# Splitting the even row frequencies once more in a gated attention and spectral mixer, with folds through PSUM, gates on ScalarE and another search of the order

## The chip, the cores and the metric

The kernel runs on one core of a Trainium2 chip. The metric is the device time of one execution in microseconds (us); the number given for a kernel is the median of its runs. A profile is one further execution under the hardware profiler.

## The reference, cut to what matters

```python
x = A_x                                   # (1, 2048, 640), float32
g = sigmoid((x * gate_w).sum(-1, keepdims=True))
# a: 32 heads of 20, each position looks at itself and 7 earlier ones, 2 apart
qkv = x @ A_wqkv                          # 640 -> 1920
logits = q . k[pos - 2*w] * 20**-0.5      # w = 0..7
a = (softmax(logits) @ v[pos - 2*w]) @ A_wo
# b: filter in the 2-D frequency domain
b = irfft2(rfft2(x, axes=(-2, -1)) * (B_w_r + 1j * B_w_i), s=(2048, 640))
out = g * a + (1 - g) * b
```

## The kernel before, in words

The position s is 16 p + j, with p on the 128 partitions and j = 0..15. Attention couples only positions of the same parity of j, so there are two parities of everything.

**The order of the work** is not written out. Every operation goes through `Plan.record` (line 222), which notes what it reads and writes, and a cost. `Plan.order` (line 278) then makes a fixed order for all engines by a list schedule forwards and backwards, and repeats it `AGAIN` = 100 times with the operations' priorities moved at random, each name of a tile by one amount over the whole program; it keeps the best by its own estimate. Because all instructions are issued from one place, the profile gives them all one line, L639, and a reader goes by the names of tiles.

**Stages.** 

- *qkv* (line 703): for 16 positions j and 4 groups of heads, 15 matmuls of 480 or 482 columns (three products of split high and low halves for each of five slices of 128 channels) into a PSUM bank from `BP`, seven banks in turn. ScalarE evicts a bank into `ev` (two buffers, each for two j) and a store to `qkvd` in HBM follows. For the first group of heads, ScalarE also copies the column `z`, the gate's argument. The very first product (`qkv<-st`) is in plain single precision from tiles `st0` (x, then the first slice of the weights), `st1`, `st2` (the other slices); `load_x` and `load_chunk` (lines 674 to 701) load them.
- *fold* (line 824): the spectral branch first folds x along the 640 channels, so that even and odd frequencies, and cosines and sines, are separate products of half the length. Each of eight folds takes two j (`fx`, with a scratch tile `fe`): six operations with both operands in SBUF, folds 0 to 6 on VectorE, fold 7 on GpSimd. The results are stored to HBM (`fd`) and come back later (`f`).
- *cols* (line 849): products with `fc`, the transform along p, into `z`, copied into `zg`.
- *attend* (line 743), two halves for each of 8 units by parity: VectorE multiplies q and k windows (`pr`, the q copied into PSUM by ScalarE as `qbank`) and reduces (`L`), a softmax, GpSimd multiplies with v windows (`pv`), VectorE reduces (`o`), and SyncE stores `od`.
- *gates* (line 735): `g`, `ng` and `nng`, three small tiles of 128 x 16, from `z`.
- *freq* (line 871), 16 groups g of row frequencies: `zc` is gathered from `zg`; `v` and `u` are products with the channel transform `bt`, three matmuls each, of 321, 161 and 160 columns; `ab` is their sum and difference; `xa` to `xd`, the transform along j; the product with the filter `wp`; the sums `s`; and `g`, back along j, into `zg`.
- *project_even* (line 1078): `ot` is read back, transposed (`oTp`, `oT`) and multiplied with `wo` (`woa` and `wob`, 15 matmuls each); results to HBM (`ad`).
- *spatial* (line 996): for each j, `o1` and `o2` (`oa`, `ob` in the profile), products with `gt`, back along the channels: three matmuls each, of 322, 161 and 161 columns; then `ha`, `hb` along p. For even j VectorE forms y from `ha`, `h`, and `yi` is added on GpSimd.
- *project_odd* (line 1094): for odd j, y from `ho` by five operations on GpSimd (`ODD_POOL`, line 1136), then the projection `woa`, `wob` and its addition. These projections come last; they need the attention of the odd parity.

Of the kernel before, what the change touches and what calls it, by code (L numbers as in the profile page):

```python
# [16 lines left out]
S, D = 2048, 640  # L17
# [7 lines left out]
PERM = np.array([0, 320] + list(range(2, 320, 2)) + list(range(1, 320, 2)))  # L25

BP = (0, 1, 2, 3, 4, 5, 6)
BV, BU, BX, BG, BO = (0,), (1, 2), (3, 4), (5,), (6,)
# [3 lines left out]
def dft_tables():  # L32
# [7 lines left out]
    ke, ko = PERM[:161], PERM[161:]  # L40
    kb = PERM[2:161]
# [9 lines left out]
    def half(n, *ends):  # L51
# [3 lines left out]

    bt = np.zeros((640, 642))
    bt[0:161, 0:161] = np.cos(tau * np.outer(np.arange(161), ke) / D) * half(161, 0, 160)
    bt[161:321, 161:321] = np.cos(tau * np.outer(np.arange(160), ko) / D) * half(160, 0)
    bt[321:480, 323:482] = -np.sin(tau * np.outer(np.arange(1, 160), kb) / D)
    bt[480:640, 482:642] = -np.sin(tau * np.outer(np.arange(1, 161), ko) / D) * half(160, 159)  # L60
    bt = np.concatenate(
        [bt[0:128, 0:161], bt[128:256, 0:321], bt[256:384, 161:482], bt[384:512, 321:642], bt[512:640, 482:642]], 1
    )

    j, k2 = np.arange(16), np.arange(16)
    md = np.zeros((16, 16, 2, 4, 2, 16, 4))
    mf = np.zeros((16, 2, 16, 4, 16, 2, 4))
    for g in range(16):
        for a in range(4):
            th = tau * np.outer(j, 4 * g + a + 128 * k2) / 2048  # L70
# [48 lines left out]
    d = np.arange(161)  # L119
# [5 lines left out]
    gt[0:161, 0:161] = np.cos(tau * np.outer(ke, d) / D) * ck(ke)  # L125
    gt[161:321, 161:322] = np.cos(tau * np.outer(ko, d) / D) * ck(ko) * (d < 160)
    gt[321:480, 322:483] = -np.sin(tau * np.outer(kb, d) / D) * ck(kb) * ((d > 0) & (d < 160))
    gt[480:640, 483:644] = -np.sin(tau * np.outer(ko, d) / D) * ck(ko) * (d > 0)
    gt = np.concatenate(
        [gt[0:128, 0:161], gt[128:256, 0:322], gt[256:384, 161:483], gt[384:512, 322:644], gt[512:640, 483:644]], 1  # L130
    )
    f = np.float32
    return {
        "t_fc": np.concatenate([fc, back[0].T, back[1].T], 1).astype(f),
# [21 lines left out]
class Plan:  # L156
# [121 lines left out]
    def order(self):  # L278
# [26 lines left out]
        for _ in range(AGAIN):  # L305
            move = MOVE * rng.choice([0.3, 1.0, 2.0]) * rng.normal(size=len(names))
            move *= rng.random(len(names)) < rng.choice([0.1, 0.5, 1.0])
            for op, t in zip(ops, (best[1] + move[family]).tolist()):
                op.tail = t
# [162 lines left out]
TURNS, AGAIN, MOVE, SEED = 6, 100, 2.0, 2  # L472
# [33 lines left out]
class Mixer:  # L506
# [17 lines left out]
    def places(self, pp, dr, sb):  # L524
# [35 lines left out]
        self.yr, self.yir = ring("raw3", "raw4", "e0", "ya"), n("f", 2)  # L560
# [10 lines left out]
    def work(self):  # L571
# [14 lines left out]
        self.qkv(0, 0)  # L586
# [4 lines left out]
        self.qkv(1, 0)  # L591
        for hg in (1, 2, 3):
            self.load_w(None, hg)
            self.qkv(0, hg)
# [13 lines left out]
        self.bt, self.gt = self.one("bt", 1288, tag="e0"), self.one("gt", 1288, tag="e1")  # L608
        S.dma_start(self.bt[:, 0:1284], ins["t_bt"])
# [16 lines left out]
        p.chain = ""  # L626
        staged([self.spatial(j) for j in range(1, NJ, 2)], 2)
# [75 lines left out]
    def qkv(self, par, hg, between=None):  # L703
# [3 lines left out]
        for jj in range(8):  # L707
            j = 2 * jj + par
            hi, lo = self.xT[j]
            b = self.ps(BP, f"qkv{u}_{jj}")  # L710
# [113 lines left out]
    def fold(self, q):  # L824
        p = self.p
        G = p.dve if q in FOLD_DVE else p.pool
# [4 lines left out]
        e = self.er.next(f"fe{q}", 2, 321)  # L831
        f, o = xt[:, :, 0:640], xt[:, :, 0:321]
        rv = xt[:, :, 640:319:-1]
# [37 lines left out]
    def freq(self, g):  # L871
# [30 lines left out]
        row(u, 1, bt[:, 161:482], True, False)  # L902
        row(u[:, 0:161], 0, bt[:, 0:161], False, False)
        row(u[:, 161:321], 2, bt[:, 482:642], False, True)
# [50 lines left out]
        V.tensor_sub(s[:, d0 : d0 + 319], P[:, 0, 2:], sz[:, 2:])  # L955
# [40 lines left out]
    def spatial(self, j):  # L996
# [8 lines left out]
        mm(o1[:, 0:322], 1, gt[:, 161:483], True, False)  # L1005
        mm(o1[:, 0:161], 0, gt[:, 0:161], False, False)
        mm(o1[:, 161:322], 2, gt[:, 483:644], False, True)
        mm(o2[:, 0:322], 3, gt[:, 805:1127], True, False)
        mm(o2[:, 0:161], 2, gt[:, 644:805], False, False)
        mm(o2[:, 161:322], 4, gt[:, 1127:1288], False, True)  # L1010
        os = self.osr.next(f"os{j}", 644)
# [188 lines left out]
```

## Time and profile before

| | us |
|---|---|
| three runs, median (lowest to highest) | 456.38 (456.13 to 456.60) |
| the profiled execution | 457.05 |
| its span, first to last instruction | 455.2 |
| granted TensorE clock | 1.0 |

In the profile PE is TensorE's matmuls, PEld its weight loads, DVE VectorE, ACT ScalarE, POOL GpSimd, SP SyncE; ACTq and SPq are the queues' own instructions, the issue of DMAs. A row of the timeline is the start of a piece, its length, engine, line, operation, the tiles written and read (out<-in), shapes, how many instructions were merged, and in brackets how long the engine stood idle before and what ended that. Matmuls overlap with their neighbours, so that what one costs is read from start to start. A row of waits is who waited for whom, us in total, times, the longest one. The rest of the time of an execution, 457.05 less 455.2, lies around the span.

### The profile page before, as it was taken

What the parts mean: (1) busy time and instruction counts of PE and PEld (TensorE: products, weight loads), DVE (VectorE), ACT (ScalarE), POOL (GpSimd) and SP (SyncE); (2) the same over time, 40 slices, a digit from 0 to 9 for tenths busy, and PEclk for the clock granted to TensorE, in tenths of its full rate; (3) what the DMA queues carried; (4) which work ended last, traced back from release to release, by engine and by line L of the source; (5) the groups of instructions that cost most, each with busy time, mean ns of one, the idle gap of its engine ahead of it and who ended that gap; (6) DMA issues with size and microseconds to landing.
All of it is one profiled execution on the core that took longest, in us unless ns stands there. A gap on an engine that the chain in (4) does not pass through costs nothing.

```text
span 455.2 us, 7081 instructions
## 1 busy us (share of the span) xinstructions
PE 444.1 (98%) x2437; PEld 390.1 (86%) x2437; DVE 408.0 (90%) x499; ACT 211.0 (46%) x562; POOL 344.2 (76%) x299
## 2 busy tenths in 40 slices
PE   8999999999999999999998999999999999999996
PEld 4888888888888888988987789878988999998996
DVE  4499999899999999999999999999999999799433
ACT  4734162424413223344367888786765563342120
POOL 1394056799999878998949894958597688888794
PEclk9999999999999999999999999999999999999999
DMA  8999998766636829989898666756653331255842
GB/s 303 411 398 295 380 355 286 238 192 224 199 95 216 267 67 268 374 261 324 241 362 291 199 213 193 265 178 200 204 160 120 88 98 57 80 189 182 274 147 87
DMA packets 70307, 102.20 MB, mean 224 GB/s; under 512 B 20464, under 2 KB 48240, under 8 KB 70272
## 3 DMA queue, kind: packets, MB, share of 16 engines
q1 hardware_dynamic: 38464, 66.20, 43.4%
q10 hardware_dynamic: 31760, 35.48, 24.1%
q8 instruction: 19, 0.31, 0.3%
q14 instruction: 16, 0.13, 0.1%
q0 software_dynamic: 48, 0.07, 0.0%
HBM read 68.90 MB, written 32.84 MB: 223 GB/s over the span
## 4 chain that ended last, share of the span: by engine, by line
DVE 44%; PE 25%; DMA 15%; issue 7%; POOL 4%; ACT 3%; ACTq 1%; SPq 0%; DVEq 0%; POOLq 0%
DMA qkvd<-ev 7%; PE woa L639 6%; PE wob L639 5%; PE g L639 2%; PE oa L639 2%; DVE xd L639 2%; PE ob L639 2%; PE u L639 2%; PE v L639 2%; DVE fx L639 1%; POOL pv0b L639 1%; DMA xt<-in_xT 1%; DMA od<-o1b 1%; DMA st<-in_w 1%; PE oTp L639 1%
## 5 line engine op out<-in xcount | busy, mean ns | idle before, releaser
L639 PE MATMUL qkv<-w,xo 128*128 128x480 f32 (+1 forms) x480 | 115.8, 388 | 0.0
L639 PE MATMUL qkv<-w,xe 128*128 128x480 f32 (+1 forms) x465 | 103.5, 382 | 0.0
L639 PEld LDWEIGHTS qkv<-w,xe 128*128 128x128 f32 x465 | 87.6, 188 | 14.6 <-issue 0.2
L639 PEld LDWEIGHTS qkv<-w,xo 128*128 128x128 f32 x480 | 89.1, 189 | 12.6
L639 PE MATMUL woa<-wo,oT 128*128 128x320 f32 x240 | 50.9, 319 | 0.0
L639 PE MATMUL wob<-wo,oT 128*128 128x320 f32 x240 | 50.8, 318 | 0.0
L639 ACT COPY ev<-qkv 128x480 f32<-128x480 f32 x64 | 35.3, 556 | 32.2 <-DMA qkvd<-ev 15.8
L639 PEld LDWEIGHTS wob<-wo,oT 128*128 128x128 f32 x240 | 39.0, 188 | 0.7 <-ACT ya L639 0.3
L639 PEld LDWEIGHTS woa<-wo,oT 128*128 128x128 f32 x240 | 38.9, 189 | 0.5
L639 POOL TENSOR_TENSOR w<-raw,w 128x480 fp32r<-128x480 f32 x15 | 19.5, 1328 | 26.2 <-ACT w L639 25.7
L639 POOL TENSOR_TENSOR P<-X,wp 128x642 f32<-128x642 f32 x16 | 24.9, 1558 | 17.3 <-ACT X L639 17.2
L639 ACT CAST oT<-oTp 128x384 fp32r<-128x384 f32 (+1 forms) x32 | 13.5, 427 | 29.8 <-PE oTp L639 17.6
L639 PEld LDWEIGHTS g<-mm,s 128*128 128x128 f32 x150 | 21.6, 190 | 6.3 <-issue 1.9
L639 POOL TENSOR_TENSOR xo<-xt,xo 128x640 fp32r<-128x640 f32 x8 | 14.6, 1857 | 16.4 <-ACT xo L639 16.4
L639 DVE TENSOR_TENSOR oT<-oTp,oT 128x384 fp32r<-128x384 f32 (+1 forms) x32 | 15.1, 485 | 12.1 <-ACT oT L639 11.9
L639 PE MATMUL g<-mm,s 128*128 128x128 f32 x150 | 24.2, 279 | 1.5 <-DVE s L639 0.7
L639 PE MATMUL oa<-gt,zg 128*128 128x161 f32 (+1 forms) x96 | 23.0, 344 | 0.0
L639 PE MATMUL v<-bt,zc 128*128 128x321 f32 (+2 forms) x96 | 22.4, 345 | 0.4 <-ACT zc L639 0.4
L639 PE MATMUL u<-bt,zc 128*128 128x321 f32 (+2 forms) x96 | 22.7, 344 | 0.0
L639 PE MATMUL ob<-gt,zg 128*128 128x161 f32 (+1 forms) x96 | 22.6, 344 | 0.0
L639 PEld LDWEIGHTS z<-fc,f 128*128 128x128 f32 x120 | 19.1, 191 | 1.5
L639 DVE TENSOR_TENSOR fx<-fx 128x642 f32<-128x642 f32 (+2 forms) x21 | 19.7, 975 | 0.3
(299 smaller groups left out, 1105.9 us busy)
## 6 DMA issues: line engine op xcount, KB each, us to landing
qkvd<-ev ACTq DMA_DIRECT2D x32, 480.0 KB, 4.7
wp<-in_ws SPq DMA_DIRECT2D x16, 642.0 KB, 4.5
fx<-in_x SPq DMA_DIRECT2D x8, 641.0 KB, 8.5
ot<-od SPq DMA_DIRECT2D x16, 320.0 KB, 3.2
fd<-fx ACTq DMA_DIRECT2D x6, 640.0 KB, 9.2
f<-fd SPq DMA_DIRECT2D x6, 640.0 KB, 5.9
raw<-in_wqkv SPq DMA_DIRECT2D x15, 240.0 KB, 5.5
xt<-in_xT SPq DMA_DIRECT2D x8, 320.0 KB, 6.4
```

What stands on the lines that cost most here:

```text
L639: p.dve.memset(w, 0.0)
```

## The change

- **Tables.** The even frequencies are split once more, into 2 mod 4 and 0 mod 4. In `freq` one of the three matmuls of `v` and one of `u` has 81 columns in place of 161 (the others 321 and 160, as before). In `spatial` odd j use a new table `g4`, with matmuls of 324, 81 and 162 columns; even j keep `gt` (322, 161, 160). `g4` is loaded into the place of `bt` when that was read last.
- **Folds** 0 to 6 now need more steps: ScalarE copies the two halves of the reversed row into PSUM (`feh`, `flo`), and 14 operations on VectorE follow, each with one operand in PSUM, and one small one on ScalarE. They use PSUM banks 4 to 6 (`BF`), so the first three units of qkv have only banks 0 to 3 (`BQ`). Fold 7, on GpSimd, has ten operations.
- **Gates**: the three additions and multiplications are on ScalarE; VectorE keeps the reciprocal.
- **Odd rows**: y takes seven operations and not five; those of j = 13 and 15 are on VectorE.
- **The search** of the order runs 250 times, and each time moves priorities only near a random time (30, 100 or 500 us to both sides).

```diff
+BQ, BF = (0, 1, 2, 3), (4, 5, 6)
...
-            for op, t in zip(ops, (best[1] + move[family]).tolist()):
+            a = rng.uniform(0, span)
+            width = rng.choice([30.0, 100.0, 500.0])
+            near = np.abs(np.array([op.start for op in ops]) - a) < width
+            for op, t in zip(ops, (best[1] + move[family] * near).tolist()):
...
-TURNS, AGAIN, MOVE, SEED = 6, 100, 2.0, 2
+TURNS, AGAIN, MOVE, SEED = 6, 250, 2.0, 2
...
-        self.qkv(0, 0)
+        self.qkv(0, 0, banks=BQ)
...
+        self.g4 = self.one("g4", 1134, tag="e0")
+        self.p.sp.dma_start(self.g4, ins["t_g4"])
...
-        p.dve.tensor_scalar_add(self.g, self.g, 1.0)
+        p.act.add(self.g, self.g, 1.0)
         p.dve.reciprocal(self.g, self.g)
-        p.dve.tensor_scalar_sub(self.nng, self.g, 1.0)
-        p.dve.tensor_scalar(out=self.ng, in0=self.g, scalar1=-1.0, scalar2=1.0, op0=ALU.mult, op1=ALU.add)
+        p.act.add(self.nng, self.g, -1.0)
+        p.act.mul(self.ng, self.nng, -1.0)
...
-        G.tensor_add(e, o, rv)
-        G.tensor_sub(o, o, rv)
-        G.tensor_sub(f[:, :, 321:480], o[:, :, 1:160], o[:, :, 319:160:-1])
-        G.tensor_add(f[:, :, 480:640], o[:, :, 1:161], o[:, :, 319:159:-1])
-        G.tensor_add(f[:, :, 0:161], e[:, :, 0:161], e[:, :, 320:159:-1])
-        G.tensor_sub(f[:, :, 161:321], e[:, :, 0:160], e[:, :, 320:160:-1])
+            p.act.copy(eh, rv[:, :, 160:321])
+            p.act.copy(bl, rv[:, :, 0:161])
+            V.tensor_sub(oh, o[:, :, 160:321], eh)
+            V.tensor_add(eh, o[:, :, 160:321], eh)
+            V.tensor_add(e, o[:, :, 0:161], bl)
+            V.tensor_sub(o[:, :, 0:161], o[:, :, 0:161], bl)
+            V.tensor_add(f[:, :, 480:640], o[:, :, 1:161], oh[:, :, 159::-1])
+            ah, al = bl[:, :, 0:80], o[:, :, 0:80]
+            V.tensor_sub(ah, o[:, :, 80:160], oh[:, :, 80:0:-1])
...
-        row(v, 4, bt[:, 803:1124], True, False)
-        row(v[:, 0:161], 3, bt[:, 642:803], False, False)
-        row(v[:, 161:321], 5, bt[:, 1124:1284], False, True)
+        row(v, 4, bt[:, 643:964], True, False)
+        row(v[:, 240:321], 3, bt[:, 562:643], False, False)
+        row(v[:, 0:160], 5, bt[:, 964:1124], False, True)
...
+        if j % 2:
+            g4 = self.g4
+            mm(o1[:, 0:324], 1, g4[:, 162:486], True, False)
+            mm(o1[:, 0:81], 2, g4[:, 486:567], False, False)
+            mm(o1[:, 162:324], 0, g4[:, 0:162], False, True)
...
-ODD_POOL = tuple(range(1, 16, 2))
+ODD_POOL = (1, 3, 5, 7, 9, 11)
```

Since the search makes the order anew, instructions move on every engine. Three places matter to the prediction. SyncE's queue at the program's start, before; `st0` is the first position of x, in two pieces, `st1` and `st2` hold slices of the first weights, `st3` and later ones further positions of x:

```order
L639 DMA st0_85<-in_xT 128x512
L639 DMA st0_85<-in_xT 128x128
L639 DMA st1_86<-in_w0 128x482
L639 DMA st3_88<-in_xT 128x640
L639 DMA st2_87<-in_w0 128x482
```

The same queue at the start now:

```order
L671 DMA st1_86<-in_w0 128x482
L671 DMA st3_88<-in_xT 128x640
L671 DMA st0_85<-in_xT 128x128
L671 DMA st0_85<-in_xT 128x512
L671 DMA st2_87<-in_w0 128x482
```

The two pieces of the first position moved from the first two places to the third and fourth. ScalarE's queue before, where the last casts of the odd x (`xo`) meet the third pair of evictions (`ev0_4`):

```order
L639 CAST xo13_138<-xt13_139 128x640
L639 CAST xo15_140<-xt15_141 128x640
L639 COPY ev0_4_105<-qkv0_4_104 128x6x80
L639 COPY z_72<-qkv0_4_104 128x1
L639 COPY ev0_4_105<-qkv0_5_106 128x6x80
L639 DMA qkvd_64<-ev0_4_105 128x6x160
```

The same place of ScalarE's queue now; `feh0` and `flo0` are the halves in PSUM of fold 0, `feh1` and `flo1` those of fold 1:

```order
L671 CAST xo15_161<-xt15_162 128x640
L671 COPY feh0_113<-fx0_110 128x322
L671 COPY flo0_112<-fx0_110 128x322
L671 COPY z_72<-qkv0_4_104 128x1
L671 COPY ev0_4_105<-qkv0_4_104 128x6x80
L671 ACTIVATE fx0_110<-flo0_112 128x2
L671 COPY z_72<-qkv0_5_106 128x1
L671 COPY ev0_4_105<-qkv0_5_106 128x6x80
L671 COPY flo1_117<-fx1_115 128x322
L671 COPY feh1_118<-fx1_115 128x322
L671 DMA qkvd_64<-ev0_4_105 128x6x160
```

Fold 0's copies stand in front of the third pair of evictions and fold 1's behind both of them. TensorE's queue at the end of the frequency groups now, from the last reads of `bt` on:

```order
L671 MATMUL u15_810<-bt_308,zc15_807 128x321
L671 MATMUL u15_810<-bt_308,zc15_807 128x81
L671 MATMUL u15_810<-bt_308,zc15_807 128x160
L671 MATMUL oTp0_859<-ident_69,ot8_857 128x128 x3
L671 MATMUL xc14_814<-ab14_796,mm13_775 128x321
L671 MATMUL g12_0_797<-mm10_729,s12_787 128x128 x3
L671 MATMUL oTp3_860<-ident_69,ot8_857 128x128 x2
```

The last `u` is followed by the remaining transforms and by `woa8` and `wob8`, 30 products, ahead of the first `oa` that reads `g4`.

More of the change, by code (lines that the diff above doesn't have):

```diff
@@ L69, in dft_tables @@
         for a in range(4):
-            th = tau * np.outer(j, 4 * g + a + 128 * k2) / 2048
+            th = tau * np.outer(j, 4 * g + a + 128 * kk) / 2048
             c, s = np.cos(th), np.sin(th)
@@ L590, in work @@
             self.load_x(None, self.xr.next(f"xo{j}", 2, 5, 128, dtype=F32R), j)
-        self.qkv(1, 0)
+        self.qkv(1, 0, banks=BQ)
         for hg in (1, 2, 3):
             self.load_w(None, hg)
-            self.qkv(0, hg)
+            self.qkv(0, hg, banks=BQ if hg == 1 else BP)
             if hg == 1:
@@ L701, in load_x, with qkv @@
         p.chain = ""
-    def qkv(self, par, hg, between=None):
+    def qkv(self, par, hg, between=None, banks=BP):
         p, d = self.p, self.qkv_d
@@ L709, in qkv @@
             hi, lo = self.xT[j]
-            b = self.ps(BP, f"qkv{u}_{jj}")
+            b = self.ps(banks, f"qkv{u}_{jj}")
             terms = []
@@ L825, in fold @@
         p = self.p
-        G = p.dve if q in FOLD_DVE else p.pool
+        V = p.dve
         xt = self.one(f"fx{q}", 2, 641, tag=FOLDS[q])
@@ L1003, in mm @@
             T.matmul(o, zg[:, t, j], r, start=start, stop=stop, skip_group_check=True)
[L1005 to L1011, printed above, removed]
+        if j % 2:
[3 more added lines that the diff above has]
+            mm(o1[:, 162:324], 0, g4[:, 0:162], False, True)
+            mm(o2[:, 0:324], 3, g4[:, 648:972], True, False)
+            mm(o2[:, 81:162], 2, g4[:, 567:648], False, False)
+            mm(o2[:, 162:324], 4, g4[:, 972:1134], False, True)
+        else:
+            mm(o1[:, 0:322], 1, gt[:, 160:482], True, False)
+            mm(o1[:, 0:161], 2, gt[:, 482:643], False, False)
+            mm(o1[:, 161:321], 0, gt[:, 0:160], False, True)
+            mm(o2[:, 0:322], 3, gt[:, 804:1126], True, False)
+            mm(o2[:, 0:161], 2, gt[:, 643:804], False, False)
+            mm(o2[:, 162:322], 4, gt[:, 1126:1286], False, True)
+        w = 162 if j % 2 else 161
+        os = self.osr.next(f"os{j}", 4 * w)
         oq = os.rearrange("p (b a d) -> p a b d", b=2, a=2)
-        A.copy(oq[:, 0], o1[:, 0:322].rearrange("p (b d) -> p b d", b=2))
-        A.copy(oq[:, 1], o2[:, 0:322].rearrange("p (b d) -> p b d", b=2))
+        A.copy(oq[:, 0], o1[:, 0 : 2 * w].rearrange("p (b d) -> p b d", b=2))
+        A.copy(oq[:, 1], o2[:, 0 : 2 * w].rearrange("p (b d) -> p b d", b=2))
         yield
```

119 lines of the change are left out of this document (85 added, 34 removed).

## The prediction

> **What bounds the kernel now.** I read the page's first part, then busy time by stretch, then the waits of each engine, then single pieces of the timeline. The first part gives TensorE nearly the whole span and VectorE little less:
>
> ```profile
> span 455.2 us, 7081 instructions
> PE 444.1 (98%) x2437; PEld 390.1 (86%) x2437; DVE 408.0 (90%) x499; ACT 211.0 (46%) x562; POOL 344.2 (76%) x299
> ```
>
> A share of 98% could be overlap only, so the stretches matter (columns: stretch in us, its length, then busy us and count of PE, PEld, DVE, ACT, POOL, then clock and DMA):
>
> ```profile
> 20.00:54.00 34.00, 34.00 (x156) 29.12 (x155) 31.97 (x37) 12.63 (x33) 17.86 (x10) 1.00 1.00 357
> 54.00:152.00 98.00, 98.00 (x451) 84.47 (x450) 94.85 (x83) 35.16 (x98) 80.93 (x64) 1.00 0.72 236
> 159.00:231.00 72.00, 72.00 (x400) 64.35 (x399) 71.23 (x61) 27.60 (x76) 63.52 (x49) 1.00 0.82 259
> 231.00:245.00 14.00, 12.29 (x70) 10.23 (x69) 14.00 (x14) 9.63 (x26) 8.11 (x8) 1.00 1.00 375
> 245.00:343.00 98.00, 94.95 (x573) 81.74 (x572) 92.19 (x157) 74.81 (x209) 76.80 (x66) 1.00 0.64 203
> 343.00:411.00 68.00, 68.00 (x429) 62.07 (x427) 64.49 (x84) 32.68 (x85) 55.36 (x47) 1.00 0.33 102
> 411.00:456.00 45.00, 39.72 (x277) 38.99 (x275) 22.62 (x47) 6.26 (x15) 32.89 (x44) 1.00 0.50 168
> ```
>
> TensorE has no idle time from 20 to 231 us and from 343 to 411. It is short of work by 1.7 us (14.00 less 12.29) as the frequency stage begins and by 3.1 us inside that stage. So the end moves with three things only: when TensorE's unbroken stream begins, how long the stream is, and those few waits. VectorE is no spare resource either: from 20 to 411 us these stretches leave it about 15 us idle, and the even outputs and the attention that the last projections need come from it. Who ends TensorE's waits in the frequency and spatial stages shows which engine is next:
>
> ```profile
> PE xa L639 <- DVE ab L639: 1.3, 1, 1.3
> PE g L639 <- DVE s L639: 0.7, 1, 0.7
> ```
>
> These are the longest, and both name VectorE. I therefore follow two paths, TensorE's stream and VectorE's queue, and ask of each edit what it does to both.
>
> **The change, part by part. Narrow products.** Each of the 16 frequency groups loses 80 columns in one product of v and one of u (161 becomes 81), and each of the 8 odd positions in one of o1 and one of o2. A single-precision product stands in the trace as two records, so 2 x (32 + 16) = 96 records shrink. What a record of 161 and one of 128 columns cost, read from start to start, in two stretches of TensorE's timeline:
>
> ```profile
> 310.48 0.60 PE L639 MATMUL g<-mm,s 128*128 128x128 f32 x4
> 310.92 0.71 PE L639 MATMUL xc<-ab,mm 128*128 128x321 f32 x2
> ...
> ```
> ```profile
> 404.06 0.71 PE L639 MATMUL ha<-os,fct 128*128 128x161 f32 x4
> 404.61 0.58 PE L639 MATMUL hb<-os,fct 128*128 128x161 f32 x3
> ```
>
> 161 columns: 0.55 over 4 is 0.137 us; 128 columns: 0.44 over 4 is 0.110. If time goes by columns alone, 81 cost 0.137 x 81/161 = 0.069, and the gain is 96 x 0.068 = 6.5 us. But every record also loads its own 128x128 weights, and no record of this kernel comes closer to its neighbour than about 0.110; if the load sets that, the gain is 96 x 0.027 = 2.6 us. I take 2.6, since 0.110 is the nearest thing measured, and keep 6.5 as the other end. Against the change speaks what the Trainium skill's page "TensorE: Matmul & The Clock Gate" says under "LDWEIGHTS (loading the stationary operand)": a load takes about the number of columns of the weights over 1.2, in ns, whatever else; that is an estimate of 107 ns for 128, so by it the narrow records would save 96 x 0.030 = 2.9 us and not 6.5. The extra column of the odd positions (324 for 322, 162 for 161) is under 0.1 us in all, at nothing.
>
> **The beginning.** SyncE's queue, shown with the change, issues the first transfers in another order: the piece of x that the first real product reads goes from the first two places to third and fourth. How TensorE begins, and, from the chain that ended last, how long a transfer that was issued third took:
>
> ```profile
> 1.06 2.93 PE L639 MATMUL warmed<-warm 128*128 128x128 f32 x12 [1.06 <-DVE warm L639]
> 4.80 1.95 PE L639 MATMUL qkv<-st 128*128 128x482 f32 x2 [0.81 <-DMA st<-in_xT]
> 6.54 4.96 PE L639 MATMUL qkv<-st,st 128*128 128x482 f32 x8
> 10.96 1.40 PE L639 MATMUL qkv<-w,xe 128*128 128x482 f32 x4
> ```
> ```profile
> 1.67 6.09 DMA st<-in_w
> ```
>
> Third in its queue landed at 7.76. The new piece is smaller than that one, so the first product begins between 4.80 (no delay) and 7.8 instead of at 4.80; I take 6.8, 2.0 later. The ten slow records behind it (4.80 to 10.96) move along, and TensorE's stream, full until 231, begins 2.0 us later: +2.0, between 0 and +3.0.
>
> **Folds.** Before, six folds of six wide operations fill VectorE from 21.59 to 53.04 us (first row of the first fold; first row of the attention):
>
> ```profile
> 21.59 1.20 DVE L639 TENSOR_TENSOR fe<-fx 128x642 f32<-128x642 f32 x1 [3.98 <-DMA fx<-in_x]
> 22.82 5.68 DVE L639 TENSOR_TENSOR fx<-fx 128x642 f32<-128x642 f32 x3
> ...
> 53.04 1.48 DVE L639 TENSOR_TENSOR pr0a<-kt0a,qbank 128x1280 f32<-128x1280 f32 x1
> ```
>
> Three operations took 5.68 us there while GpSimd was in its own work. Now a fold is 14 operations with an operand in PSUM, 6 long and 8 short. Rows of that kind, by their starts, are these:
>
> ```profile
> 276.55 0.88 DVE L639 TENSOR_TENSOR ab<-u,vs 128x321 f32<-128x321 f32 x2
> 277.35 0.41 DVE L639 TENSOR_REDUCE m5b<-L5b 128x32 f32<-128x256 f32 x1
> ```
> ```profile
> 399.92 0.38 DVE L639 SCALAR_TENSOR_TENSOR h<-ha,ng,h 128x161 f32<-128x161 f32 x1
> 400.21 0.38 DVE L639 SCALAR_TENSOR_TENSOR h<-ha,nng,h 128x160 f32<-128x160 f32 x1
> ```
>
> 0.40 and 0.29 us: 6 x 0.40 + 8 x 0.29 = 4.7 us a fold (by full durations, 0.48 and 0.38, 5.9), against (53.04 - 21.59)/6 = 5.2 before. That alone would gain 3 us. But each fold now waits for two copies on ScalarE, and these stand in ScalarE's queue among the evictions of qkv. As the pieces of that queue shown with the change have it, fold 0 comes behind the last cast of xo, fold 1 behind the third eviction buffer. ScalarE's timeline before, at these two instructions:
>
> ```profile
> 23.82 1.99 ACT L639 CAST xo<-xt 128x640 fp32r<-128x640 f32 x3 [0.45 <-ACT z L639]
> 32.91 0.56 ACT L639 COPY ev<-qkv 128x480 f32<-128x480 f32 x1 [7.11 <-DMA qkvd<-ev]
> ```
>
> The casts end at 25.8, so fold 0 runs 26.2 to 31.0 (0.4 for a copy, as in the 0.56 of a 480-wide one). The eviction waits for its buffer's store until 32.9, and fold 1 starts at about 34.4. Folds 2 to 5 follow at 4.7, each with some 0.4 us for copies that may only start when the banks of the fold before are free: 34.4 + 5 x 4.7 + 4 x 0.4 = 59.5, 6.5 later than 53.04. The ends: 26.2 + 6 x 4.7 = 54.4 if nothing waits (+1.4), and 34.4 + 5 x 5.9 + 1.6 = 65.5 (+12.5). Behind that, VectorE has 2.5 us of waits in the attention before 90 us that swallow some of it:
>
> ```profile
> DVE pr0a L639 <- ACT qbank L639: 1.3, 1, 1.3
> DVE pr4a L639 <- ACT qbank L639: 1.2, 1, 1.2
> ```
>
> VectorE is then 4.0 later (between -1.1 and +10). The qkv products of this stretch also get four banks in place of seven; at 15 records of 0.217 us (451 in the 98 us from 54) a group is 3.26 us, so a copy may come 9.8 us after its group before TensorE stops. I cost that at nothing, with up to 2 if ScalarE's queue slips further.
>
> **Gates.** On VectorE's timeline the small tensor-scalars sit for microseconds:
>
> ```profile
> 152.06 0.99 DVE L639 TENSOR_SCALAR g<-g 128x16 f32<-128x16 f32 x1
> 153.09 0.25 DVE L639 RECIPROCAL g<-g 128x16 f32<-128x16 f32 x1
> 153.37 3.80 DVE L639 TENSOR_SCALAR ng<-g 128x16 f32<-128x16 f32 x1
> 154.28 2.91 DVE L639 TENSOR_SCALAR nng<-g 128x16 f32<-128x16 f32 x1
> 154.35 2.84 DVE L639 TENSOR_TENSOR pr2a<-kt2a,qbank 128x1280 f32<-128x1280 f32 x1
> 157.25 1.49 DVE L639 TENSOR_REDUCE L2a<-pr2a 128x64 f32<-128x1280 f32 x1
> ```
> ```profile
> 152.97 4.17 POOL L639 TENSOR_TENSOR pv1a<-vt1a,L1a 128x640 f32<-128x640 f32 x3
> ```
>
> They end at 157.17, GpSimd's three products at 157.14. From 152.06 to 157.25 are 5.2 us; the reciprocal (0.25) and pr2a (1.48 in its other rows, as L2a's 1.49) stay, so VectorE gains 3.5. The Trainium skill's page "SBUF — State Buffer", under "Who interferes with whom", has these two engines lock each other out of a shared port pair, for tensor-scalar forms and for two inputs in SBUF; here the trace agrees for the gates (157.17 and 157.14). By the rule alone the folds, now with one input in SBUF, would gain and nothing speaks against them; the queue on ScalarE is what I set against that.
>
> **The rest.** Two odd rows' sums go from GpSimd to VectorE (about 2.5 us each, 14 operations in all), under the 22 us that VectorE idles behind 411; if that cover went, up to 5. The new table g4 is loaded behind the last group's reads of bt, while TensorE still has two 15-product blocks of the even projection to run; nothing. The search of the order is longer and local; what it can win is TensorE's waits from 231 on, 1.7 + 3.1 + about 1.5 behind 411, and I take 2.5 of these 6 (from none to all, or 3 lost).
>
> **Sum**, against the profiled execution of 457.05 us (span 455.2): products -2.6, beginning +2.0, waits -2.5; VectorE +4.0 - 3.5 = +0.5 later, which returns as TensorE's waits. Together -2.6. From the median of 456.38 that is **453.8 us**.
>
> **Rivals.** Each is from the median.
> - *Time by columns.* The weight loads hide and 81 columns cost 0.069: -6.5 + 2.0 - 2.5 + 0.5 = -6.5, **449.9**. For it: loads overlap the wide records. Against: 0.110 is the closest spacing seen.
> - *ScalarE's queue holds the folds* (slower). Fold 5 ends at 59.5 or later, nothing swallows it as the two later waits move along, and 6.5 - 3.5 = +3.0 stays with VectorE; the attention ends 3.0 later and the odd projections, about 40 us of products, with it, so TensorE's saved columns become waits: **459.4**. It decides from the point where fold 5 ends behind 59.0 (53.04 + 3.5 + 2.5). For it: the 7.11 us wait; against: a store that lands sooner.
> - *Nothing to see.* The later beginning eats the columns, VectorE is even, the new order wins nothing: -2.6 + 2.0 + 0.5, **456.3**.
>
> **How the numbers follow.** Forecast 0.37, time by columns 0.18, ScalarE's queue 0.28, nothing to see 0.17. 0.2% (0.9 us) is about what a measurement of this kernel can tell from no change. Faster is the first two, 0.55; same 0.17; slower 0.28. The range leaves out the outer part of each end: 449.5 (all columns) to 460.0 (the queue, with some stop of TensorE).
>
> **What would show it.** Right: narrow records 0.110 apart; first qkv product near 6.8; fold 5's end near 59.5; no microsecond gates. Wrong: first product at 4.8, narrow records near 0.07, a fold end by 55, or TensorE idle between 36 and 65 us for its banks.

## The result, and the profile after

The changed kernel takes 462.68 us (median of four runs, 461.46 to 463.28) against 456.49 for the kernel before beside it: a ratio of 1.0127, with a 95% interval of 1.0102 to 1.0152. It is slower, and above the predicted range of 449.5 to 460.0. The profiled execution took 461.46, its span is 459.4; it is the fastest of the four, with a mean granted clock of 0.996 against 0.990 to 0.992 in the others. The page's first part, of the changed kernel:

```profile
span 459.4 us, 7200 instructions
PE 443.8 (97%) x2437; PEld 388.8 (85%) x2437; DVE 408.9 (89%) x566; ACT 220.0 (48%) x586; POOL 341.8 (74%) x305
```

TensorE is as busy as before (444.1), and idle for 15.6 us of the span instead of 11.1. Busy time by stretch tells where (columns as in the prediction):

```profile
20.00:54.00 34.00, 31.23 (x141) 26.50 (x141) 23.29 (x63) 16.68 (x44) 15.88 (x11) 0.99 0.94 334
...
231.00:245.00 14.00, 14.00 (x88) 12.59 (x87) 13.64 (x13) 8.26 (x23) 8.63 (x9) 1.00 0.92 319
245.00:343.00 98.00, 94.65 (x568) 80.16 (x567) 92.15 (x157) 76.54 (x211) 79.07 (x69) 1.00 0.71 229
343.00:411.00 68.00, 67.26 (x431) 61.31 (x430) 66.14 (x84) 33.54 (x88) 56.97 (x48) 1.00 0.37 114
411.00:460.00 49.00, 43.54 (x304) 42.72 (x303) 31.18 (x66) 8.20 (x20) 35.44 (x47) 0.99 0.49 158
```

The unbroken stream has a hole of 2.8 us between 20 and 54 us, and VectorE did 23.29 us of work there instead of 31.97. From 231 us on little changed: TensorE idles 9.0 us up to the end of the span, and idled 9.3 before. How TensorE begins now, on its timeline:

```profile
6.84 1.94 PE L671 MATMUL qkv<-st 128*128 128x482 f32 x2 [2.85 <-DMA st<-in_xT]
8.57 1.81 PE L671 MATMUL qkv<-st,st 128*128 128x482 f32 x2
...
13.52 2.73 PE L671 MATMUL qkv<-w,xe 128*128 128x482 f32 x10
```

The first product comes at 6.84, the quick stream at 13.52 instead of 10.96. The hole, on the same timeline, and the clock around it (length, TensorE's busy time and count, granted clock, DMA):

```profile
39.80 10.03 PE L671 MATMUL qkv<-w,xo 128*128 128x482 f32 x45
52.61 11.93 PE L671 MATMUL qkv<-w,xo 128*128 128x482 f32 x46 [2.77 <-ACT ev L671]
```
```profile
45.00:49.60 4.60, 4.60 (x23) 1.00 0.98 275
49.60:52.60 3.00, 0.23 (x2) 1.00 0.99 384
53.30:56.70 3.40, 3.40 (x11) 0.50 1.09 388
57.00:60.00 3.00, 3.00 (x16) 1.00 1.02 403
```

TensorE waits 2.77 us for ScalarE's copy of a bank. Then the clock is halved (0.50 in the third row): eight products come 0.40 us apart instead of 0.22, which is another 1.5 us. ScalarE's timeline shows why the copy (the last row) is late; ACTq is the issue of a DMA in the same queue:

```profile
46.66 1.51 ACTq L671 DMA_DIRECT2D q0b<-qkvd  x1
48.35 0.17 ACT L671 ACTIVATE fx<-flo 128x2 f32<-128x2 f32 x1 [2.17 <-DVE fx L671]
48.41 1.75 ACTq L671 DMA_DIRECT2D vt0a<-qkvd  x1
50.20 0.69 ACTq L671 DMA_DIRECT2D vt0b<-qkvd  x1
50.94 0.43 ACT L671 COPY flo<-fx 128x322 f32<-128x322 f32 x1 [2.42 <-DVE fx L671]
51.30 0.42 ACT L671 COPY feh<-fx 128x322 f32<-128x322 f32 x1
51.52 0.38 ACTq L671 DMA_DIRECT2D fd<-fx  x1
51.93 0.16 ACT L671 COPY z<-qkv 128x1 f32<-128x1 f32 x1 [0.20 <-issue]
51.99 0.56 ACT L671 COPY ev<-qkv 128x480 f32<-128x480 f32 x1
```

The copy's group of products, `qkv4_2`, had ended at 48.7 us. The copy stands behind three loads for attention, a doubling that waits for VectorE's fold, the next fold's copies and a store. And TensorE wants that bank soon: in its queue the groups of the odd positions (`qkv4_`, then a number) begin in the order 0, 1, 2, 4, 6, 5, 3, 7. The four banks go round by number, so that `qkv4_6` takes the bank of `qkv4_2`, and between the end of the one and the start of the other stand only five products of `qkv4_4`, until 49.84. `qkv4_3` and `qkv4_5`, whose banks ScalarE had copied by 46.2 us, wait behind it. The folds on VectorE's timeline (starts of folds 0, 1 and 4, and what follows fold 5):

```profile
27.21 0.50 DVE L671 TENSOR_TENSOR foh<-fx,feh 128x322 f32<-128x322 f32 x1 [6.12 <-ACT feh L671]
...
34.36 0.49 DVE L671 TENSOR_TENSOR fe<-fx,flo 128x322 f32<-128x322 f32 x1 [1.93 <-ACT flo L671]
...
51.40 0.49 DVE L671 TENSOR_TENSOR fe<-fx,flo 128x322 f32<-128x322 f32 x1 [1.06 <-ACT flo L671]
...
64.47 1.48 DVE L671 TENSOR_TENSOR pr0a<-kt0a,qbank 128x1280 f32<-128x1280 f32 x1
```

Fold 0 starts at 27.2 instead of 21.6, and fold 5 ends at 64.5, with one product of attention and its sum (2.9 us) inside. The narrow products and the gates look as meant; two pieces of the frequency stage, then ScalarE's gates:

```profile
291.55 0.35 PE L671 MATMUL v<-bt,zc 128*128 128x81 f32 x2
291.74 0.43 PE L671 MATMUL g<-mm,s 128*128 128x128 f32 x2
292.00 0.44 PE L671 MATMUL v<-bt,zc 128*128 128x160 f32 x2
```
```profile
110.65 0.21 ACT L671 ACTIVATE nng<-g 128x16 f32<-128x16 f32 x1
110.89 0.21 ACT L671 ACTIVATE ng<-nng 128x16 f32<-128x16 f32 x1
```

The two narrow records take 0.19 us from start to start. Over all 48 pairs the first stands 0.071 us from the second and the second 0.111 from what follows, a mean of 0.091 (0.136 for 161 columns).

### The profile page after: what moved, and what is told of

It is laid out like the page before. It is cut to its first block, busy times and chain, and to the rows that moved or that the text cites. A ratio compares the mean times of both kernels' runs of the same rounds, so it can differ in the third digit from the quotient of the medians.

```text
span 459.4 us, 7200 instructions
## 1 busy us (share of the span) xinstructions
PE 443.8 (97%) x2437; PEld 388.8 (85%) x2437; DVE 408.9 (89%) x566; ACT 220.0 (48%) x586; POOL 341.8 (74%) x305
## 4 chain that ended last, share of the span: by engine, by line
PE 56%; DVE 15%; POOL 12%; DMA 7%; issue 4%; ACT 3%; ACTq 1%; POOLq 0%; DVEq 0%
PE qkv L671 37%; PE z L671 4%; DMA qkvd<-ev 3%; POOL ye L671 3%; PE u L671 3%; PE g L671 3%; POOL yi L671 2%; POOL pv7b L671 2%; PE v L671 2%; POOL pv7a L671 2%; PE xc L671 2%; PE woa L671 2%; PE xa L671 2%; POOL y L671 2%; DVE fx L671 2%
## 5 line engine op out<-in xcount | busy, mean ns | idle before, releaser
L671 PE MATMUL qkv<-w,xo 128*128 128x480 f32 (+1 forms) x480 | 120.1, 393 | 2.8 <-ACT ev L671 2.8
L671 PE MATMUL qkv<-w,xe 128*128 128x480 f32 (+1 forms) x465 | 106.1, 384 | 0.0
L671 PE MATMUL woa<-wo,oT 128*128 128x320 f32 x240 | 53.5, 315 | 0.0
L671 PE MATMUL wob<-wo,oT 128*128 128x320 f32 x240 | 53.2, 314 | 0.0
L671 POOL TENSOR_TENSOR xo<-xt,xo 128x640 fp32r<-128x640 f32 x8 | 12.3, 1586 | 18.4 <-ACT xo L671 18.4
L671 PE MATMUL v<-bt,zc 128*128 128x321 f32 (+2 forms) x96 | 20.4, 336 | 0.3 <-ACT vs L671 0.3
L671 PE MATMUL u<-bt,zc 128*128 128x321 f32 (+2 forms) x96 | 20.6, 337 | 0.0
L671 ACT COPY zg<-z 128x512 f32<-128x512 f32 (+1 forms) x24 | 11.8, 518 | 14.6 <-PE z L671 14.4
L671 PEld LDWEIGHTS v<-bt,zc 128*128 128x128 f32 x96 | 15.2, 191 | 3.9 <-ACT vs L671 0.8
L671 PE MATMUL z<-fc,f 128*128 128x128 f32 x120 | 17.9, 274 | 0.0
```

The source lines that it names most:

```text
L671: p.dve.memset(w, 0.0)
```

## The experiments

Eighteen kernels, measured in five batches; every ratio is the recorded one against the kernel before in the same batch (its median was 456.5 to 457.1), and differs from the quotient of the two medians by up to 0.23%. "Stop" is TensorE's longest idle time between 30 and 75 us in the profile, "idle" all of its idle time between 20 and 75 us (none in the kernel before).

| kernel | median us | ratio (95%) | stop us | idle us |
|---|---|---|---|---|
| changed | 462.68 | 1.0127 (1.0102-1.0152) | 2.77 | 2.8 |
| e_start | 463.43 | 1.0128 (1.0090-1.0165) | 4.45 | 6.4 |
| e_copy | 460.47 | 1.0062 (1.0039-1.0085) | 2.97 | 3.7 |
| e_both | 461.20 | 1.0093 (1.0064-1.0122) | 2.70 | 5.5 |
| e_mul | 459.34 | 1.0048 (1.0029-1.0067) | 1.56 | 1.6 |
| e_full | 460.53 | 1.0085 (1.0062-1.0107) | 1.14 | 3.1 |
| e_vec | 461.91 | 1.0128 (1.0099-1.0158) | 4.70 | 5.6 |
| e_idle | 459.56 | 1.0032 (1.0002-1.0062) | 2.12 | 2.1 |
| e_idle_s | 457.40 | 1.0014 (0.9997-1.0031) | 3.03 | 3.9 |
| e_less | 462.03 | 1.0115 (1.0098-1.0132) | 2.54 | 2.5 |
| e_gback | 462.67 | 1.0128 (1.0105-1.0151) | 4.49 | 4.5 |
| e_seed | 464.46 | 1.0169 (1.0145-1.0194) | 3.58 | 5.5 |
| e_sbuf | 464.55 | 1.0185 (1.0152-1.0219) | none | 0 |
| e_psum | 459.83 | 1.0073 (1.0049-1.0098) | 0.30 | 0.3 |
| e_psum3 | 461.82 | 1.0097 (1.0080-1.0114) | 0.80 | 1.6 |
| e_search | 455.94 | 0.9969 (0.9949-0.9990) | none | 0 |
| e_search3 | 456.98 | 1.0004 (0.9979-1.0030) | none | 0 |
| e_gates | 454.62 | 0.9953 (0.9927-0.9980) | none | 0 |
| e_banks | 454.41 | 0.9939 (0.9914-0.9964) | 0.83 | 1.5 |

### The order edited by hand: e_start, e_copy, e_both, e_mul, e_full, e_vec

These keep the changed kernel's searched order and move single instructions in it, by their places in the list: `START` is a permutation of the first 76, and `moved` sorts each engine's instructions by the places that `HOLD` gives (a number is an instruction's old place, behind it the new one).

```diff
         order = self.order()
+        order[:76] = [order[i] for i in START]        # e_start, e_both, e_full, e_vec
+        order = moved(order, HOLD)                    # all but e_start
+HOLD = {335: 369.3, 343: 369.4, 347: 369.5, 355: 369.1, 360: 369.2, 363: 369.6}   # e_copy, e_both
```

> The changed kernel with its first loads, copies and products put back in the order of the kernel before (first 76 places of the order; all else stays). Theory, that TensorE's stream was set back by its late start and by the stop for a bank: the first qkv product starts near 4.8 us instead of 6.84, the stream of short products near 11.0 instead of 13.52, and the time falls by 2.0 to 2.5 us, from 462.7 to 460.2-460.7. Rival, that VectorE's later folds set the time: the start moves alike, the time by less than 0.7 us.

> The changed kernel with six of ScalarE's instructions (the DMA issues q0b, vt0a, vt0b and fd of fold 3, the copies flo4 and feh4) put behind the copy of the third odd qkv group, that TensorE's next group waits for; all else stays. Theory of TensorE's set-backs: the stop of 2.8 us at 49.8-52.6 us goes, the clock stays at 1.00 behind it, qkv record 200 starts near 55.5 us instead of 59.98, and the time falls by 3.5 to 4.3 us, to 458.4-459.2. Rival, VectorE's folds: the stop goes, fold 5 still ends near 63-64.5 us, and the time falls by less than 1.5 us.

> Both edits of the order at once. Theory of TensorE's set-backs: they add, 5.5 to 6.8 us, 455.9 to 457.2, that is no change against the kernel before, and the gain in the frequency stage (2.4 us between the last record of attention's products and the last g) shows as 0 to 1 us under it. Rival, VectorE's folds: 461 or more, less than 2 us gained.

In e_start the first product came at 4.05 and the stream at 9.8, and nothing was gained: TensorE only came earlier to the same banks, whose copy came at 52.7 us (52.0 in the changed kernel).

```profile
43.55 5.33 PE L675 MATMUL qkv<-w,xo 128*128 128x482 f32 x23 [1.39 <-ACT ev L675]
53.32 11.93 PE L675 MATMUL qkv<-w,xo 128*128 128x482 f32 x46 [4.45 <-ACT ev L675]
```

e_copy took away most of the stop near 50 us (0.69 is left), but another one of the same size came 11 us later. TensorE's row of it, and what holds ScalarE there:

```profile
63.20 0.93 PE L687 MATMUL qkv<-w,xo 128*128 128x482 f32 x3 [2.97 <-ACT z L687]
```
```profile
59.56 0.21 ACT L687 COPY L0a<-low 1x16 f32<-1x16 f32 x1 [1.14 <-DVE L0a L687]
62.46 0.17 ACT L687 ACTIVATE fx<-flo 128x2 f32<-128x2 f32 x1 [2.69 <-DVE fx L687]
62.53 0.55 ACT L687 COPY ev<-qkv 128x480 f32<-128x480 f32 x1
```

The doubling of one column pair waits 2.69 us for VectorE's fold 5, with the copies of two banks behind it. The median fell by 2.2 us, the profiled span by 0.7 only. In e_both three waits for copies remain, 5.0 us in all, and 1.5 us of the median are gained where 5.5 to 6.8 were expected. The next three take the doubling away too; in them VectorE does it:

```diff
+        for op in [o for o in order if o.name == "mul" and o.of.startswith("fx")]:
+            op.eng, op.call[1]["fn"] = "DVE", tc.nc.vector.tensor_scalar_mul
+            HOLD[at[op]] = max(at[q] for q in op.preds) + 0.5
+HOLD |= {150: 118.1, 154: 118.2}                          # e_full, e_vec: feh0, flo0 earlier
+HOLD |= {200: 186.1, 204: 186.2, 246: 220.1, 253: 220.2, 409: 460.1, 418: 460.2}  # e_vec
```

> e_copy, and in each fold on VectorE the doubling of one column pair (fx<-flo, 128x2), which ScalarE did in the middle of the fold, is done by VectorE itself, at the place where its operand is ready; the rest of the order stays. Second theory, that ScalarE's queue ties the copies that free the four banks to the folds (the doubling waits for VectorE with the copies behind it): the stop of 2.97 us before 63.20 us in e_copy falls under 1 us, the clock stays at 1.00 there, qkv record 250 starts at 66.5 to 68.5 us instead of 70.78, and the time falls by 2.5 to 4.5 us from e_copy's 460.5, to 456.0-458.0. Rival, VectorE's folds set the time themselves: record 250 earlier by the same, the time by less than 0.8 us.

> e_mul, with the beginning of e_start too, and with the two ScalarE copies of the first fold (feh0, flo0) put ahead of four of the casts of odd rows that they stood behind. Second theory: the first fold starts near 23.5 us instead of 27-28, no stop for a bank over 1 us before 71 us, record 250 at 64.5 to 66.5 us, and the time is 453.5 to 456.5, at or under the kernel before. Rival, VectorE: attention starts 2 to 4 us earlier, too, so a gain here doesn't tell the two apart by itself; but a time over 459 speaks against both.

> e_full with ScalarE's copies for the second and third fold put ahead of the qkv copies that wait for a transfer's landing (33.89 and 36.85 us), and the first product of attention and its sum behind the sixth fold. It tells VectorE's lateness apart from TensorE's stops, since e_full has hardly any stop left and is still behind. Third theory, that after its idle time at 20-40 us VectorE is late for good (o0b ends 6 us later in every variant so far) and the end follows it: the second fold starts near 30.5 us instead of 35.34, the sixth ends at 57.5-59 us instead of about 64, o0b ends 3 to 4 us earlier than 129.37, and the time falls by 2 to 4 us from e_full's 460.5, to 456.5-458.5. Rival, TensorE's stream alone: VectorE gets there earlier, and the time changes by less than 1 us.

e_mul is the best of this group: 3.3 us under the changed kernel, a stop of 1.56 and no halved clock behind it, but not the 456.0 to 458.0 that were expected. e_full has no stop over 1.14 us in this stretch and is not better: by its own expectation, 460.53 speaks against both theories. Its 457.7 us of span still holds 15.5 us of idle TensorE, and the waits of about 1 us between 20 and 75 us come to 3.1. e_vec put attention's first product and sum behind fold 5, and ScalarE's next copies behind them, so that TensorE stood for 4.70 us; it doesn't tell VectorE's part. So each edit of ScalarE's queue gave the wait to another copy.

### The work that VectorE has: e_less, e_gback, e_idle, e_idle_s

All in the changed kernel's own order (e_idle_s with `START`). e_less and e_idle leave work out, so that columns stay unfolded.

```diff
             for op in order:
+                if op.eng == "DVE" and op.of.split("_")[0] in ("fe6", "flo6", "feh6", "foh6", "fx6"):
+                    continue                                   # e_less
+                if name[:-1] in ("fe", "flo", "feh", "foh", "fx") and name[-1] in "012345":
+                    if op.eng == "DVE" or op.name == "mul":
+                        continue                               # e_idle, e_idle_s
                 exec(*op.call)
+            if op.eng == "ACT" and (op.of[:2] == "g_" and op.name == "add" or op.of[:3] in ("nng", "ng_")):
+                op.eng, op.call[1]["fn"] = "DVE", getattr(v, "tensor_scalar_" + op.name)    # e_gback
```

> The changed kernel in its own order, with the 14 VectorE operations of the seventh fold left out (5.1 us of VectorE between 75.59 and 85.04 us; the columns of that fold are then not folded). It leaves TensorE's start and its stop at 49.8-52.6 us untouched. Third theory, that VectorE's lateness carries to the end: o0b ends near 124.5 instead of 129.53, and the time falls by 3 to 5 us from 462.7, to 457.7-459.7. Rival, TensorE's set-backs alone: 461.7 or more, under 1 us gained.

> The changed kernel in its own order, with the three small operations of the gates given back to VectorE at the same places (two at 64 and 102 us of the plan, one behind it). Third theory: VectorE loses 2.5 to 3.5 us in its full stretch, the time rises by 1.5 to 3.5 us, to 464.2-466.2. Rival, TensorE alone: no change within 0.8 us.

> The changed kernel in its own order, with the VectorE operations and the doubling of folds 0 to 5 left out (their columns stay unfolded); ScalarE's copies for them stay in its queue and wait for a transfer alone. It takes ScalarE's waits for VectorE away and nothing else that TensorE waits for. If TensorE's stop in the folds' stage is the loss: no stop for a bank over 1 us before 71 us, qkv record 250 at 66 to 67.5 us instead of 70.96, and 457.5 to 459.5, 3 to 5 us under the changed kernel's 462.7. If the loss lies behind that stage: 461.5 or more.

> e_idle with the beginning of e_start as well. In e_start the earlier beginning was eaten by longer stops (6.4 us for a copy); with no fold in ScalarE's way it should count: record 250 at 64 to 65.5 us, and 455 to 457.5, 1.5 to 2.5 us under e_idle. If an early beginning counts for nothing by itself, as in the kernel before with other orders: within 0.8 us of e_idle.

4.9 us less on VectorE (e_less) changed nothing that can be measured, nor did 1.6 us more, which is all that the gates cost when given back (e_gback). VectorE's waits in e_less say what its freed time turned into (who waits, for whom, us in total, times, longest; the changed kernel has neither row):

```profile
DVE pr0b L675 <- ACT qbank L675: 3.0, 1, 3.0
DVE pr4a L675 <- ACT qbank L675: 1.8, 1, 1.8
```

Attention's pace is set by the copies of q, that is by ScalarE, the loads and the qkv products ahead of them. e_idle is the sharpest: VectorE has 29.5 us less to do,

```profile
span 457.4 us, 7087 instructions
PE 442.8 (97%) x2437; PEld 388.4 (85%) x2437; DVE 379.4 (83%) x482; ACT 219.0 (48%) x580; POOL 341.4 (75%) x305
```

and the span falls by 2.0 us. Just as much, 1.9, does record 250 of the qkv products, counted from 0, come earlier (69.06 for 70.96). So TensorE's stream sets the end. The other kernels of these two groups say the same, since TensorE's queue is alike in all ten but for two places at the start. At the product that the changed kernel starts at 79 us, e_start is 0.7 us behind it and e_gback 1.6, e_vec 0.8 ahead, e_idle 1.9 and e_idle_s 2.0; at the last product they are 0.9 and 1.7 behind, 1.0, 1.9 and 2.1 ahead. e_copy, e_both and e_less are within 0.2 us of it at 79 us and within 0.6 at the end. Only e_mul, 3.8 ahead at 79 us, and e_full, 3.5, lose most or part of it on the way, to 0.5 and 2.1, in waits of up to 1.3 us between 90 and 270 us. What the changed kernel loses it has thus lost by 79 us.

But the stop is still there in e_idle, with no fold to wait for; TensorE, then ScalarE:

```profile
50.71 11.93 PE L677 MATMUL qkv<-w,xo 128*128 128x482 f32 x46 [2.12 <-ACT ev L677]
```
```profile
49.62 0.38 ACTq L677 DMA_DIRECT2D fd<-fx  x1
50.03 0.16 ACT L677 COPY z<-qkv 128x1 f32<-128x1 f32 x1 [2.44 <-DMA q0a<-qkvd]
50.09 0.56 ACT L677 COPY ev<-qkv 128x480 f32<-128x480 f32 x1
```

The copy stands behind a store's issue, which uses the same semaphore as the load q0a and began, at 49.62, only when that had landed, at 49.59. ScalarE's queue is thus held by two things, folds and DMA issues, and my claim for e_idle, no stop over 1 us, failed. Two of its ten runs took 454.4 and 454.9, the others 459.2 to 460.3. The two had a mean granted clock of 1.000, the others 0.992 to 0.996. The runs of e_copy and e_both part alike, 458.1 to 459.3 at 1.000 and 460.2 to 464.1 below it, those of e_mul do not. So in three kernels the executions without a halved clock are some 2 to 5 us faster; no trace of such an execution was kept, so that its stops are not known. The earlier beginning in e_idle_s brought record 250 forward to 68.95 only, where 64 to 65.5 was expected. Its median is 2.2 us under e_idle's, as expected, but the intervals do not part the two.

### One part alone: e_search, e_search3, e_gates, e_banks, e_psum, e_psum3, e_sbuf, e_seed

Here the order is searched anew. The first four are the kernel before with the new search and at most one part more; e_psum and e_psum3 are e_banks with the folds' form as well. e_seed is the changed kernel, and e_sbuf the changed kernel without PSUM in the folds and with seven banks.

```diff
+            near = np.abs(np.array([op.start for op in ops]) - a) < width     # e_search and all below
+TURNS, AGAIN, MOVE, SEED = 6, 250, 2.0, 2                  # 3 in e_search3, e_psum3, e_seed
+        p.act.add(self.g, self.g, 1.0)                     # e_gates: the three on ScalarE
+            self.qkv(0, hg, banks=BQ if hg == 1 else BP)   # e_banks, e_psum: four banks as changed
+            p.act.copy(eh, rv[:, :, 160:321])              # e_psum: folds through PSUM, one split
+            G = V if q in FOLD_DVE else p.pool             # e_sbuf: folds as GpSimd's, seven banks
```

> The kernel before with the new search of the order alone (local moves, 250 instead of 100), its work unchanged. Theory of TensorE's set-backs, by which they come from the four banks and one choice at the start: 455 to 458, within 1.5 us of before. Rival, that the new search itself chooses worse orders: 459.5 or more, with a first qkv product late (6 us or more) here too.

> The kernel before with the new search from another seed (3). It sizes the luck of one order: two seeds of the kernel before within 3 us of each other, 454 to 459, and both under the two of the changed kernel (1.0127 and 1.0169 of before). A time of 460 or more would say that luck alone spans the difference.

> The kernel before with the new search (e_search) and the gates' three small operations on ScalarE instead of VectorE, nothing else. The prediction's term: 3.5 us leave VectorE. If VectorE's time counts in full: 452.5, 3.5 us under e_search's 455.9. If TensorE's stream sets the end: 455 to 456.5, no change against e_search.

> The kernel before with the new search (e_search) and four banks instead of seven for the same qkv groups as in the changed kernel; its folds stay out of PSUM and off ScalarE. Second theory, that the banks cost only together with folds in ScalarE's queue: 455 to 457, under 1 us more than e_search's 455.9, with no stop of TensorE over 1 us for a copy. Rival, four banks are too few by themselves: stops of 2 us or more before 71 us, and 458 or more.

> e_banks with the folds' form of the changed kernel alone: mirrored half copied to PSUM by ScalarE, two levels instead of three, no doubling on ScalarE; one split of the row frequencies as before, gates on VectorE. If ScalarE's copies ahead of the folds are what sets VectorE back: VectorE is busy under 13 of the 20 us at 20-40 (18.1 in e_banks), and the time is 457.5 to 460, 3 to 5 us over e_banks' 454.4. If the loss needs the longer folds of the second split: 453.5 to 456.

> e_psum, its order searched from another seed (3). If the folds' form costs by itself and not the luck of one order: 457.5 to 462, over all four orders of the kernel before (0.9939 to 1.0004 of it). If e_psum's order was unlucky: 454 to 457.

> The changed kernel with the folds on VectorE taken out of PSUM and off ScalarE (both operands in SBUF, as GpSimd's fold has them, ten operations), and seven banks for all qkv groups again; the second split, the gates, the odd rows and the search stay, and the order is searched anew. If the folds' form is the whole loss: first fold near 21.5-22 us, no stop for a bank over 1 us, and with the narrow products' 2 us the time is 452 to 454.5, under e_gates' 454.6. If the split costs by itself (longer folds beside GpSimd, odd rows with one operation more): 457 or more.

> The changed kernel, its order searched from another seed (3 instead of 2). If its work sets the time: 459 to 464, with the first fold after 25 us and a stop of TensorE for a bank of over 1 us between 36 and 71 us again. If the one order was unlucky: 454 to 457.5.

Four kernels without folds through PSUM lie from 0.9939 to 1.0004; that is the luck of a searched order, and the new search, the gates and the four banks alone cannot be told apart inside it; e_gates, at 454.62, lies between its two expectations. e_search begins late too, its first product at 6.64 and its quick stream at 13.00, and is no slower than the kernel before. Four banks alone stop TensorE little (its waits in e_banks):

```profile
PE qkv L643 <- ACT ev L643: 1.1, 2, 0.8
PE qkv L643 <- ACT z L643: 0.4, 1, 0.4
```

The folds' form alone costs: 1.0073 and 1.0097, two orders, both over all four. And this although it spares VectorE 10.7 us. First the page of e_banks, then that of e_psum:

```profile
PE 443.6 (98%) x2437; PEld 389.0 (86%) x2437; DVE 407.9 (90%) x499; ACT 213.0 (47%) x562; POOL 343.4 (76%) x299
```
```profile
PE 445.0 (97%) x2437; PEld 390.0 (85%) x2437; DVE 397.2 (87%) x513; ACT 217.4 (48%) x576; POOL 339.2 (74%) x299
```

It isn't by a stop for a bank: neither e_psum nor e_psum3 has one of 0.9 us. Of the 5.5 us between the spans of e_banks (452.0) and e_psum (457.5), 4.1 are idle time of TensorE. Its quick stream begins at 13.38 instead of 10.28, and from 231 to 343 us it idles 2.9 us more, 2.1 of them for the load of a table; e_psum3 is alike (13.36, and 3.7 more). How the folds' form leads to that isn't shown. Another order of the whole change (e_seed) is no better, so the two orders don't speak for bad luck. Its stop of 3.58 us isn't for a bank, but for a cast of weights in the same queue of ScalarE, behind a doubling that waits for VectorE; TensorE, then ScalarE:

```profile
67.69 0.77 PE L671 MATMUL qkv<-w,xe 128*128 128x480 f32 x1 [3.58 <-ACT w L671]
66.98 0.17 ACT L671 ACTIVATE fx<-flo 128x2 f32<-128x2 f32 x1 [2.72 <-DVE fx L671]
```

e_sbuf, second split without PSUM, shows the other way to lose: 8.4 us more on VectorE than the changed kernel, no stop for a bank, attention's last sum ends at 435.7 instead of 429.5, and TensorE waits 3.1 us at 420.7 for VectorE.

```profile
PE 447.8 (96%) x2437; PEld 391.1 (84%) x2437; DVE 417.3 (90%) x538; ACT 212.7 (46%) x565; POOL 344.9 (74%) x305
```

e_banks and e_gates beat both kernels, at 0.9939 and 0.9953; neither holds the second split or a fold in PSUM.

## Why the prediction was wrong, step by step

- **The four banks** are the step that failed: "I cost that at nothing, with up to 2 if ScalarE's queue slips further." The stop cost 2.77 us and 1.5 more in halved clock, 4.3 in the profile. In e_gback's profile, with the same order in this stretch, it is 4.49 us and 12 slow products, in an execution of 463.10. The reason that I gave, that a copy may come 9.8 us behind its group, holds only if the groups stand in the order of their banks. In the searched order `qkv4_6` wants the bank of `qkv4_2` 1.1 us after that group's end (48.7 to 49.8), and the copy began 3.2 us after it. I had followed neither queue there. That the copies and DMA issues in ScalarE's queue are what holds the copy is shown by e_copy, where moving six of them leaves 0.69 us of this stop, and by e_idle, where a DMA issue alone does it. But the whole loss isn't undone by moving them: e_copy and e_mul gain 2.2 and 3.3 us, and e_full is still 0.85% over the kernel before.
- **Waits by the new search**, -2.5: from 231 us on TensorE's idle time fell by 0.3. In the kernel before the same search gave -0.3% and nothing, by seed.
- **VectorE's sum**, +4.0 for the folds and -3.5 for the gates, "which returns as TensorE's waits": the sizes were about right (fold 5's end 64.5 less 2.9 for attention's work inside is 61.6, forecast 59.5; no gate takes a microsecond), the price was not. e_less, e_gback, e_idle and e_psum move VectorE's work by 1.6 to 29.5 us, and the time doesn't follow it. Only where the work grows by 8.4 us (e_sbuf) does VectorE's lateness reach the end.
- **The beginning**, +2.0: the stream begins 2.56 later, as forecast with the first product at 6.84 for 6.8. But it isn't a term to add: undone in e_start it was lost again at the next copies, which came no earlier, and in e_both, e_full and e_idle_s it is no gain that the intervals show.
- **Narrow products**, -2.6: about -2.5, and the nearness is luck. The first record of a pair goes by columns (0.071 us), and the second stands at the spacing that I took as the bound (0.111). Against 0.136 for 161 columns, 48 pairs save 3.1 and 1.2 us, and the record behind a pair takes 0.042 longer in nearly all of them (0.178 for 160 columns), 1.9 back. My 0.110, read at 128 columns, showed no bound: by columns alone they take 0.137 x 128/161 = 0.109. The 107 ns that the prediction had worked out, as an estimate, from the Trainium skill's page "TensorE: Matmul & The Clock Gate", under "LDWEIGHTS (loading the stationary operand)", are near the spacing of the second record of a pair (0.108 to 0.112) and not of the first.
- **TensorE's ledger** in the profile is then -2.5 + 2.6 + 4.3 - 0.3 = +4.1, against +4.2 of span. By record 250 of the qkv products TensorE is 6.8 us late (70.96 for 64.17), which is the beginning, the stop and the halved clock; behind that it gains 2.6. The other three runs were 0.8 to 1.8 us longer at a lower mean clock, as e_gback's profiled execution was.
- **The rivals.** "ScalarE's queue holds the folds", at 0.28, named the right engine and the right sign (459.4), but led it through VectorE and attention. The way was the sign that the list of what would prove it wrong names last: TensorE idle between 36 and 65 us for its banks.

What stays open: how the folds' form costs time without a stop (e_psum, e_psum3); why e_mul and e_full, 3.8 and 3.5 us ahead at 79 us, do not keep it; and why the second split costs some 0.5% more than the folds' form alone (1.0127 and 1.0169 against 1.0073 and 1.0097), though its products are 2.5 us shorter.

## What to carry to other kernels

When a change puts new work into the queue of an engine that also frees another engine's buffers, follow that queue instruction by instruction, its DMA issues too, and set the time at which each copy comes against the time at which its buffer is wanted. That time is read from the order in which the buffers are asked for, and not from their number: four banks left 1.1 us here and not 9.8. Engine shares (48% here) say nothing about it. Four banks alone were harmless in the order found for them (e_banks); a longer queue alone wasn't run. And count an idle gap of the full engine with the slow stretch behind it.

## What the runs showed of the hardware

- TensorE's clock after a gap: in these profiles every idle gap of TensorE between 30 and 75 us of 2.12 us or more (2.12, 2.54, 2.70, 2.77, 2.97, 3.03, 3.58, 4.45, 4.49, 4.70) was followed by 7 to 13 products at half speed, and none up to 1.56 us was. Length alone doesn't decide it: a gap of 2.13 us at 243.48 in e_psum, in the frequency stage, was followed by none. The Trainium skill's page "TensorE: Matmul & The Clock Gate" says under "HAM oscillation — how this bites in real kernels" that gaps over about 3.4 us are to be avoided; these runs show half speed after gaps from 2.12 us on.
- Two records of 81 columns of one product, each with its own 128x128 weights, stood 0.069 to 0.075 us apart. The second stood 0.108 to 0.112 from the next record, and that one took 0.042 longer than its kind elsewhere.
